# Nyström attention, ELU feed-forward and top-2 experts in one Trainium2 kernel: float32 transposes and landmark sums of batch 0 on TensorE, 32x32 Newton blocks, contiguous A parts, and a new order of all engines

## The chip, the cores and the metric

The kernel runs on one core of a Trainium2 chip. The metric is device time in microseconds (us), the median of several executions of the whole kernel; lower is better. The engines are named as the profile names them: PE is TensorE (PEld its weight loads), DVE VectorE, ACT ScalarE, POOL GpSimd, and SP the engine that issues the plain DMAs. Each engine works through its own instructions in order.

## What is computed

Three stages follow each other. Nyström attention has 4 batches, 8 heads, 576 tokens of 64 numbers and 32 landmarks, each of which is the mean of 18 successive tokens. Its output is a matrix x of 2304 tokens by 512, which goes through a feed-forward layer with ELU, and then through a router that sends each token to two of eight experts.

```python
q_lm = q.reshape(B, H, 32, 18, 64).mean(axis=3)          # same for k
A, Bm, C = sm(q, k_lm), sm(q_lm, k_lm), sm(q_lm, k)      # row softmaxes of scaled products
Z = Bm.T / (norm1(Bm) * norminf(Bm) + 1e-6)
for _ in range(6):
    Z = 2 * Z - Z @ Bm @ Z
x = A @ Z @ C @ v
h = x @ w_in                                             # 512 -> 2048
y = where(h > 0, h, exp(min(h, 0)) - 1) @ w_out          # 2048 -> 512
out = sum over the 2 best experts of weight * relu(y @ w1[e]) @ w2[e]
```

## The kernel before

**Number formats.** Most products run in float16 with every operand split into a high part and a remainder ("hi" and "lo"), three matmuls per product (hi hi, hi lo, lo hi). The splits are made by ACT (hi) and by DVE or POOL (lo). The weights w_in and w_out arrive as raw 32-bit words that four steps per tile turn into floats: `I.j.part` and `Wa.kk.part`, where part 0 runs on ACT, part 1 (line 256) and part 2 (line 257) on DVE, and part 3 on POOL (line 258). `Wb` then splits w_out into two float16 halves (line 289 on DVE).

**Attention.** Each of the 4 batches is worked on in two groups g of 4 heads. `lmsum` sums 18 tokens per landmark from the float32 q or k, on DVE (one reduction, line 318) or POOL (six additions). `xhi` (ACT) and `xlo` (DVE, line 364) split q and k. For batch 0, PE transposes the halves (`xtp`, line 370, 6 float16 blocks per call, 12 calls) and ACT or DVE copies them out of PSUM (`xte`, line 378); for batches 1 to 3 a DMA transposes them (`xtr`). The landmark sums are split (`lhi`, `llo`), transposed on PE (`ltr`) and copied out (`lcp`). Then come the three score products: `asmm` for A, `csmm` for C, `bmm` for B. A's softmax is a chain of steps between DVE, POOL and ACT (`astr`, `asmax`, `assub`, `asexp`, `assum`, `asmul`, `asback`), and its result is written as hi by ACT (`ashi`) and lo by DVE or POOL (`aslo`, line 591) into the tile AT, with a token order that strides through it.

**Newton.** The 32x32 matrices of the 8 heads are handled as block-diagonal 128x128 matrices of 4 heads. `btd` spreads the transpose of B into such blocks; `sqmm` squares one (line 452: two float32 matmuls of 128x128x128), `sqout` copies it to R, `umm` multiplies it into Y (line 524: two float32 matmuls with 32 columns), `uout` adds. Six rounds of each follow per batch. With `zcv` and `gmm`, Z, C v and w_in are folded into one matrix G per batch, whose halves are written by `ghi` (ACT) and `glo` (DVE, line 609).

**Feed-forward.** The 2304 tokens go in 6 chunks (512, 256, then four of 384), each with 16 blocks f of 128 hidden units. `L1.c.f` (line 634) forms h from AT and G, `X` takes exp on ACT, `T` the clipped part on ACT or DVE (line 656), `S` combines on DVE (line 660), `H` writes the float16 hi on ACT, `O` the lo on POOL (line 665), and `L2.c.f.t` (line 672) accumulates the outputs of 128 tokens each. The routing, the split of the expert weights and expert 0 come after; the remaining seven experts run in a loop of their own. `F.n` issues n idle matmuls of 128x128 on PE (line 646), which feed nothing.

**What sets the order.** One long string, ORDER, lists every step up to expert 0, as `batch:step.arguments` or `step.arguments`. The steps are issued in that order, and the scheduler is told to leave it alone on PE, DVE, ACT, POOL and SP, so the string fixes the row in each queue.

```python
with tc.manual_schedule(engines={ET.PE, ET.DVE, ET.Activation, ET.Pool, ET.SP}):
    do(ORDER)
```

Of the kernel before, what the change touches and what calls it, by code (L numbers as in the profile page):

```python
# [56 lines left out]
0:xtp.1.1.1 0:xte.1.1.1.A 0:nmm 0:btd.V I.7.2 0:nval Wl.7 Wa.0.0 0:sqmm.0 0:xtp.0.1.0 0:asmax.0 F.9 0:y0 I.1.1
0:xte.1.0.0.A 0:xtp.1.0.2 0:xtp.1.0.1 0:sqout.0 0:xte.1.1.2.V 0:sqmm.1 Wl.2 0:umm.0 0:xte.1.0.2.A I.3.1 wi.10
0:sqout.1 Wa.7.0 Wa.0.1 0:xtp.0.1.2 0:assub.0.G 0:xte.1.0.1.V I.7.0 I.4.1 0:sqmm.2 wi.9 0:asexp.0 I.0.3 0:csmm.1
0:sqout.2 Wa.0.2 Wl.3 I.1.2 wi.11 0:uout.0 0:csmm.0 Wa.4.3 Wa.0.3 I.3.0 Wb.0.0.V Wb.4.0.V 0:assum.0 0:xte.0.1.0.V  # L60
I.1.3 wi.12 Wa.7.1 0:xte.0.1.2.V 0:sqmm.3 0:sqout.3 0:umm.1 0:xtp.0.1.1 0:uout.1 wi.5 F.11 Wa.2.0 0:xte.0.1.1.A
0:umm.2 Wa.7.2 Wa.2.1 0:sqmm.4 F.9 0:csmax.0 0:csmax.1 Wa.1.1 Wa.2.2 Wa.1.2 Wa.7.3 0:asmul.0.G 0:csexp.0 I.11.0 I.12.0
F.10 I.2.2 0:csexp.1 Wa.3.0 I.8.1 I.11.1 0:asmm.1 I.9.0 0:uout.2 0:etrans.1 0:astr.1 0:etout.1 I.12.1 I.4.2 Wa.1.3
wi.13 Wl.5 I.4.0 0:umm.3 I.5.1 Wb.0.1.V 0:v 0:sqout.4 0:etrans.2 Wb.4.1.V 0:etrans.0 Wa.5.0 cl I.2.3 0:asmax.1 I.8.2
1:k.0 0:sqmm.5 0:sqout.5 0:uout.3 0:assub.1.G F.14 Wl.6 0:etout.2 0:asback.0 0:asexp.1 0:etout.0 Wa.2.3 Wb.1.0.V
Wb.2.0.V 0:ashi.0 0:umm.4 Wa.3.1 0:cssum I.3.2 Wb.7.0.V F.8 I.7.3 0:cv 0:uout.4 0:assum.1 0:cvout 0:umm.5 0:uout.5
I.3.3 I.4.3 I.5.0 1:q.0 0:asmul.1.V 0:ybd.V 0:aslo.0.G Wa.5.1 0:asback.1 0:zcv Wb.2.1.V 0:zout 0:ashi.1 1:lmsum.0.0.V
0:gmm.0 I.8.0 Wb.7.1.V 0:ghi.0.0 1:xhi.0.0 0:ghi.0.1 0:glo.0.1 F.36 0:aslo.1.G 0:glo.0.0 1:xlo.0.0 L1.0.0 I.10.0 X.0.0
I.5.2 T.0.0.V 1:xhi.1.0 S.0.0 L1.0.1 Wa.5.2 I.5.3 X.0.1 L1.0.2 wi.14 I.10.1 0:gmm.1 H.0.0 T.0.1.A Wa.3.2 Wb.1.1.V
O.0.0 S.0.1 1:xlo.1.0 I.13.0 L2.0.0.2 0:ghi.1.0 L2.0.0.3 X.0.2 Wa.3.3 H.0.1 0:ghi.1.1 1:q.1 1:lmsum.0.1.V L1.0.3  # L70
Wa.5.3 Wa.6.0 T.0.2.A L2.0.0.1 I.14.1 Wb.3.0.G O.0.1 S.0.2 1:lmsum.1.0.V 1:v 1:lhi.0 Wb.5.0.V X.0.3 0:glo.1.0 L2.0.0.0
L2.0.1.1 I.8.3 H.0.2 Wb.3.1.G T.0.3.A L2.0.1.0 1:xtr.0.0 0:glo.1.1 S.0.3 I.10.2 O.0.2 L2.0.1.3 1:xhi.0.1 Wb.5.1.V
1:llo.0 L1.0.5 L1.0.4 wi.15 I.9.1 consts 1:ltr.0 L2.0.2.3 I.9.2 H.0.3 1:k.1 X.0.5 O.0.3 1:lcp.0.A X.0.4 1:xlo.0.1
I.11.2 T.0.5.A I.11.3 L2.0.1.2 L2.0.2.0 T.0.4.V Wa.6.1 L2.0.3.3 S.0.4 I.9.3 L2.0.2.2 H.0.4 L2.0.3.2 I.10.3 S.0.5
L2.0.2.1 1:xtr.1.0 1:xtr.0.1 L2.0.3.1 L1.0.6 L1.0.7 O.0.4 I.14.2 I.14.0 H.0.5 1:lmsum.1.1.V 0:gmm.2 Wa.6.2 L2.0.4.3
I.15.0 1:xhi.1.1 X.0.6 0:ghi.2.1 O.0.5 0:ghi.2.0 Wa.6.3 L2.0.3.0 1:xlo.1.1 Wl.9 T.0.6.A L2.0.4.0 1:lhi.1 X.0.7
0:glo.2.0 L2.0.4.2 L2.0.5.2 S.0.6 Wb.6.0.V H.0.6 0:glo.2.1 Wl.8 Wa.9.0 O.0.6 Wa.9.1 1:llo.1 1:csmm.0 1:xtr.1.1 Wa.9.2
I.14.3 1:csmax.0 I.12.2 I.13.1 L2.0.4.1 L1.0.8 T.0.7.A Wb.6.1.V L2.0.5.3 X.0.8 Wl.12 Wa.8.1 I.15.1 1:csexp.0 L2.0.5.0
S.0.7 L2.0.5.1 L2.0.6.0 H.0.7 1:ltr.1 L2.0.6.3 T.0.8.A 1:lcp.1.V I.13.2 O.0.7 1:bmm Wa.8.2 L1.0.9 I.12.3 1:bmax Wa.8.0
X.0.9 1:csmm.1 L2.0.6.1 Wa.9.3 1:csmax.1 L2.0.6.2 L2.0.7.2 Wl.13 L2.0.7.1 1:bex T.0.9.A I.15.2 S.0.9 Wa.8.3 1:csexp.1  # L80
L2.0.7.0 I.15.3 1:asmm.0 Wa.12.0 1:bnorm 1:astr.0 L1.0.10 1:etrans.0 1:nmm I.13.3 Wl.11 Wb.8.0.V Wb.8.1.V 1:btd.A
# [95 lines left out]
EV.4.1 EA.0.1 EV.0.1 E1.2.1 EV.1.1 E1.6.1 E1.3.1 LW.0.1 EA.2.1 EA.6.1 EV.2.1 EV.6.1 LX.1.0 EA.3.1 ES.1 EA.7.1 ES.2
EV.3.1 EV.7.1 E2.3 E2.4 EO.4 PD.2.3 EO.3 LW.1.0 ES.3 ES.4
"""


# [953 lines left out]
```

## Time and profile before

| | us |
| --- | --- |
| median of 3 runs | 844.60 |
| lowest and highest of them | 843.96 and 846.16 |
| the profiled execution, its own time | 843.73 |
| its span | 842.1 |

The span is what the profile shows from the first to the last instruction, 1.6 us less than the time of that same execution. The start of the span, up to 64.4 us, is the attention of batch 0 and the first weight conversions. From 64.4 to about 150 us chunk 0 of the feed-forward runs beside the attention of batch 1; to about 450 us the other chunks run beside batches 2 and 3; and then come the experts. In the views a busy time is what an engine's instructions covered, "x" is their count, and PEclk is the granted TensorE clock as a share of full speed.

### The profile page before, as it was taken

The numbers are of one execution on the slowest core, as the hardware profiler recorded it, in microseconds if no ns is written. First come the engines' busy times: TensorE is split into PE (matmuls) and PEld (weight loads), VectorE is DVE, ScalarE is ACT, GpSimd is POOL, SyncE is SP. The second block draws the span as 40 slices with busy tenths as digits, with TensorE's granted clock in tenths as the row PEclk, the third lists the DMA queues.
The fourth block names the chain that finished last, engine by engine and source line by source line (L and its number), as shares of the span: only waits on it lengthen the run. The fifth ranks groups of instructions, "written<-read, shape, count | busy, mean of one in ns | idle before, by whom it ended". The sixth has DMA issues, their size and how long they took to land. (4 is left out here: it accounts for less than half of the span.)

```text
span 842.1 us, 15270 instructions
## 1 busy us (share of the span) xinstructions
...
## 2 busy tenths in 40 slices
...
GB/s 334 305 168 192 184 299 343 154 214 219 111 218 98 181 81 127 76 110 55 190 101 201 144 182 122 144 161 91 183 81 160 139 110 189 49 11 39 223 107 36
DMA packets 136971, 129.11 MB, mean 153 GB/s; under 512 B 100581, under 2 KB 103653, under 8 KB 136800
## 3 DMA queue, kind: packets, MB, share of 16 engines
...
HBM read 70.64 MB, written 39.90 MB: 131 GB/s over the span
## 5 line engine op out<-in xcount | busy, mean ns | idle before, releaser
L931 PE MATMUL ey<-w,eh 128*128 128x512 f16 (+1 forms) x960 | 208.8, 379 | 0.0
L672 PE MATMUL y<-wout,g 128*128 128x512 f16 x864 | 207.1, 379 | 1.6 <-DVE wout L289 0.9
L901 PE MATMUL eh<-xT,w 128*128 128x304 f16 (+2 forms) x1536 | 200.4, 293 | 0.0
L911 DVE SCALAR_TENSOR_TENSOR eh<-eh,eh 128x304 f16<-128x304 f32 (+2 forms) x128 | 59.8, 471 | 228.0 <-ACT eh L217 228.0
L901 PEld LDWEIGHTS <-w 128*128 128x128 f16 x1536 | 149.9, 98 | 49.6
L931 PEld LDWEIGHTS <-eh 128*128 128x128 f16 (+1 forms) x960 | 98.7, 103 | 106.9
L939 POOL DMA_INDIRECT acc<-eo,tk x35 | 55.9, 1597 | 280.2 <-ACT eo L217 144.1
L665 POOL TENSOR_TENSOR g<-e,g 128x384 f16<-128x384 f32 (+2 forms) x96 | 100.4, 1049 | 129.8 <-ACT g L217 113.8
L672 PEld LDWEIGHTS <-g 128*128 128x128 f16 x864 | 81.3, 99 | 94.6 <-issue 9.3
L634 PE MATMUL h<-AT,G 128*128 128x192 f16 (+3 forms) x768 | 110.2, 289 | 7.9 <-DVE e L660 5.0
L217 ACT ACTIVATE eh<-eh 128x304 f16<-128x304 f32 (+2 forms) x128 | 53.8, 424 | 118.0 <-PE eh L901 111.3
L634 PEld LDWEIGHTS <-G 128*128 128x128 f16 x768 | 64.2, 99 | 49.4 <-issue 11.2
L868 DVE SCALAR_TENSOR_TENSOR w<-ew,w 128x1024 f16<-128x1024 f32 x64 | 78.2, 1223 | 22.8 <-ACT w L217 22.8
L217 ACT ACTIVATE eo<-ey,ws 128x512 f32<-128x512 f32 (+1 forms) x35 | 23.8, 687 | 135.1 <-PE ey L931 135.1
L660 DVE SCALAR_TENSOR_TENSOR e<-e,h 128x384 f32<-128x384 f32 (+2 forms) x96 | 52.6, 550 | 33.8 <-ACT e L217 26.0
L217 ACT ACTIVATE e<-h 128x384 f32<-128x384 f32 (+2 forms) x96 | 47.4, 495 | 47.3 <-PE h L634 22.0
L217 ACT ACTIVATE w<-ew 128x1024 f16<-128x1024 f32 x64 | 66.9, 1047 | 0.0
L217 ACT ACTIVATE g<-e 128x384 f16<-128x384 f32 (+2 forms) x96 | 49.8, 520 | 31.7 <-DVE e L660 18.6
L840 POOL DMA_INDIRECT xs<-rows,pos x36 | 36.5, 1014 | 31.4 <-DVE count L832 20.5
L217 ACT ACTIVATE e<-e 128x384 f32<-128x384 f32 (+2 forms) x57 | 30.0, 526 | 0.9
L656 DVE TENSOR_SCALAR e<-e 128x384 f32<-128x384 f32 (+2 forms) x39 | 19.2, 493 | 17.0 <-ACT e L217 16.9
L609 DVE SCALAR_TENSOR_TENSOR G<-pg,G 128x512 f16<-128x512 f32 x32 | 21.6, 689 | 7.7 <-ACT G L217 7.7
...
## 6 DMA issues: line engine op xcount, KB each, us to landing
...
v<-in_v_dram SPq DMA_DIRECT2D x4, 1152.0 KB, 11.0
...
```

The costliest lines, as they stand in the source:

```text
L217: return A.activation(o, i, f, **kw)
L609: V.scalar_tensor_tensor(gt[:, g, 1, fs], X["pg"][g], S_G, gt[:, g, 0, fs], op0=ALU.mult, op1=ALU.subtract)
L634: T.matmul(p[:, c0:c0 + n], GT[b, f // 8][:, g, x, fs], AT[b][:, g, y, o:o + n], start=(i == 0), stop=(i == 5))
L660: V.scalar_tensor_tensor(x[1], x[1], x[2], x[0], op0=ALU.mult, op1=ALU.max)
L665: G.tensor_tensor(out=HT[c, f][:, 1], in0=x[1], in1=HT[c, f][:, 0], op=ALU.subtract)
L672: T.matmul(YP[c, t], h[:, x, 128 * t:128 * t + 128], WOUT[f][:, y], start=(f == 0 and i == 0), stop=(f == 15 and i == 2))
L840: n = nc.gpsimd.indirect_dma_start(out=xs[:, :], out_offset=bass.IndirectOffsetOnAxis(ap=R["pos"][:, i // 2, i % 2:i % 2 + 1], axis=0), in ...
L868: V.scalar_tensor_tensor(dst[1][:, ks, :], t, scale, dst[0][:, ks, :], op0=ALU.mult, op1=ALU.subtract)
L901: T.matmul(p, W1T[e][x][:, d, 128 * f:128 * f + 128], XT[e][y][:, d, s0:s0 + n], start=(i == 0 and d == 0), stop=(i == 2 and d == 3))
L911: V.scalar_tensor_tensor(h[:, 1, s0:s0 + n], EP[e, f, s0], 0.0, h[:, 0, s0:s0 + n], op0=ALU.max, op1=ALU.subtract)
L931: T.matmul(p, EH[e, f][:, x, 128 * j:128 * j + live(j)], W2T[e][y][:, f, :], start=(f == 0 and i == 0), stop=(f == 7 and i == 2))
L939: nc.gpsimd.indirect_dma_start(out=acc[:, :], out_offset=bass.IndirectOffsetOnAxis(ap=TK[e][:live(j), j:j + 1], axis=0), in_=EO[e, j], in_ ...
```

## The change

1. **Batch 0's inputs.** The float32 q and k are transposed directly on PE: `xtp` now makes 3 float32 blocks per call (12 calls). The split follows behind the transposition, out of PSUM: `xth` writes hi on ACT, `xtl` lo on DVE. The landmark sums of batch 0 are formed on PE too: `lmmm` adds pairs of tokens with 9 float32 matmuls against the identity, 4 calls, and `lmadd` (DVE) adds what is left. `xhi`, `xlo`, `xte` and `lmsum` are no longer used for batch 0.
2. **Newton.** `btd` is gone. `sqmm` and `umm` issue 8 matmuls of 32x32x32, one for each head, and R shrinks to 32 columns per group.
3. **A's parts** are written contiguously, so that a batch's tokens come in another order. The noise of the router is therefore loaded by 16 DMAs (`nz.b.j`) in place of one, and the token numbers take six more small DVE operations in `consts`.
4. **The remainder O** of ELU may run on DVE. Of chunk 0's 16 it does so for 11; over all chunks DVE has 54 of 96. T of chunk 0 runs on ACT throughout (before, 10 on ACT and 6 on DVE). `aslo` of batch 1 moves from DVE to POOL, and other steps of A's softmax are dealt out anew between DVE and POOL.
5. **The overflow branch**, which runs only when an expert gets more than 608 tokens, uses plain loads and a selecting matmul instead of indirect DMAs. It isn't executed on these inputs.
6. **ORDER** is written anew throughout. The first loads are weights, then k and q in turn.

```diff
-F.127 0:q.0 0:xhi.0.0 0:k.0 0:xtp.0.0.0 0:k.1 0:xhi.1.1 0:q.1 Wl.4 0:xlo.0.0 0:lmsum.0.0.G 0:lmsum.1.0.V 0:xte.0.0.0.A
...
+F.127 wi.2 wi.0 0:k.0 wi.6 0:q.0 0:xtp.0.0.0 I.0.0 0:xtp.1.0.0 I.6.0 I.0.1 0:xth.0.0.0 0:lmmm.0.0 0:q.1 I.6.1 I.6.2
...
+    ident32 = cst.tile([128, M], F32, name="ident32")
+    V.tensor_reduce(out=ident32, in_=ident.rearrange("p (h m) -> p m h", h=4), axis=AX.X, op=ALU.add)
...
+        def lmmm(s_, g):
+            x = (QS, KS)[s_][b, g]
+            p = X["ls", s_, g] = small("", None, 256 * s_ + 128 * g, 128)
+            for r in range(SEG // 2):
+                T.matmul(p, ident, x[:, 2 * D * r:2 * D * r + 2 * D], start=(r == 0), stop=(r == SEG // 2 - 1))
+        def lmadd(s_):
...
+            p = small("", None, 256 * s_, 256).rearrange("p (g u d) -> p g d u", g=2, u=2)
+            V.tensor_reduce(out=X["lmr"][:, s_], in_=p, axis=AX.X, op=ALU.add)
...
-            p = X["xp", n, g, j] = s1(f"xp{b}{n}{g}{j}", ("a", "y")[n], F16)
-            for c in range(6):
-                T.transpose(p[:, 128 * c:128 * c + 128],
-                            X["x", n, g].rearrange("p x n -> p (x n)")[:, 128 * (6 * j + c):128 * (6 * j + c + 1)], ident16)
-        def xte(n, g, j, e):
+            p = X["xp", n, g, j] = s1(f"xp{b}{n}{g}{j}", ("a", "y")[n])
+            for c in range(3):
+                T.transpose(p[:, 128 * c:128 * c + 128], (QS, KS)[n][b, g][:, 128 * (3 * j + c):128 * (3 * j + c + 1)], ident)
+        def xth(n, g, j):
...
+            act(xT[n, g][:, 3 * j:3 * j + 3].rearrange("p c n -> p (c n)"), X["xp", n, g, j][:, :384], scale=S_QK)
+        def xtl(n, g, j):
+            hi, lo = (xT[n, g][:, o + 3 * j:o + 3 * j + 3].rearrange("p c n -> p (c n)") for o in (0, 9))
+            V.scalar_tensor_tensor(lo, X["xp", n, g, j][:, :384], S_QK, hi, op0=ALU.mult, op1=ALU.subtract)
...
-        def btd(e):
-            X["BTd"] = tile_a([128, 2, 4, M], "k1")
-            spread(X["BTd"], X["BB"][:, 1], 2, e)
...
+        def blocks(p, x, y):
+            for g in range(2):
+                for h in range(4):
+                    sl = slice(32 * h, 32 * h + 32)
+                    T.matmul(p[sl, g], x[sl, g], y[sl, g], start=True, stop=True)
         def sqmm(i):
-            p = X["pq", i] = small(f"pq{b}{i}", n_tag, 0, 256).rearrange("p (g m) -> p g m", g=2)
-            for g in range(2):
-                x = X["BTd"][:, g].rearrange("p h m -> p (h m)") if i == 0 else R[i - 1][:, g]
-                T.matmul(p[:, g], x, x, start=True, stop=True)
+            p = X["pq", i] = small(f"pq{b}{i}", n_tag, 0, 64).rearrange("p (g m) -> p g m", g=2)
+            x = X["BB"][:, 1] if i == 0 else R[i - 1]
+            blocks(p, x, x)
         def sqout(i):
             p = X["pq", i]
-            r = R[i] = sa.tile([128, 2, 128], F32, tag="R", bufs=NR, name=f"R{b}{i}")
+            r = R[i] = sa.tile([128, 2, M], F32, tag="R", bufs=NR, name=f"R{b}{i}")
...
         def umm(i):
...
-            for g in range(2):
-                T.matmul(p[:, g], R[i][:, g], Y[:, g], start=True, stop=True)
+            blocks(p, R[i], X["Y"])
...
         def ashi(g):
...
-            act(AT[b][:, g, 0, :].rearrange("p (m c u) -> p u c m", u=2, c=9), X["ay", g])
+            act(AT[b][:, g, 0, :].rearrange("p (c u m) -> p u c m", u=2, c=9), X["ay", g])
         def aslo(g, e=V):
-            hi, lo = (AT[b][:, g, i, :].rearrange("p (m c u) -> p u c m", u=2, c=9) for i in range(2))
+            hi, lo = (AT[b][:, g, i, :].rearrange("p (c u m) -> p u c m", u=2, c=9) for i in range(2))
...
         if part == "O":
-            G.tensor_tensor(out=HT[c, f][:, 1], in0=x[1], in1=HT[c, f][:, 0], op=ALU.subtract)
+            e.tensor_tensor(out=HT[c, f][:, 1], in0=x[1], in1=HT[c, f][:, 0], op=ALU.subtract)
...
-        nc.sync.dma_start(noise_t, noise.rearrange("(t p) e -> p t e", p=128))
+    def noise_load(b, j):
+        r0 = (j - SEG * b) % 4
+        n, t0 = len(range(r0, SEG, 4)), (SEG * b + r0) // 4
+        nc.sync.dma_start(noise_t[32 * j:32 * j + 32, t0:t0 + n],
+                          noise.rearrange("(b m r) e -> b m r e", b=B, r=SEG)[b, :, r0::4])
```

Three places of the new order follow. In a row, a name is that of a tile, the digits behind its underscore count tiles, and the sizes are those of the output.

**The start, on DVE.** Before, rows 8 to 16 of DVE's queue; `x` holds the two float16 halves, `k10` the landmark sums, `T` the transposed halves, `lm` the split sums:

```order
L364 SCALAR_TENSOR_TENSOR x000_236<-q00_234,x000_236 128x1152
L318 TENSOR_REDUCE k10_256<-k00_238 128x64
L318 TENSOR_REDUCE k10_256<-q01_251 128x64
L378 COPY T000_266<-xp0001_268 128x768
L256 TENSOR_SCALAR woc4_277<-wo4_253 128x512
L332 SCALAR_TENSOR_TENSOR lm0_257<-k10_256,lm0_257 128x2x64 x2
L364 SCALAR_TENSOR_TENSOR x101_249<-k01_247,x101_249 128x1152
L364 SCALAR_TENSOR_TENSOR x100_290<-k00_238,x100_290 128x1152
L332 SCALAR_TENSOR_TENSOR lm0_257<-k10_256,lm0_257 128x2x64 x2
```

After, rows 11 to 21:

```order
L262 SCALAR_TENSOR_TENSOR wi12_242<-wi12_242,win1_256 128x512
L262 SCALAR_TENSOR_TENSOR wi00_238<-wi00_238,win0_250 128x512
L400 SCALAR_TENSOR_TENSOR T000_259<-xp0000_246,T000_259 128x384
L400 SCALAR_TENSOR_TENSOR T100_279<-xp0100_252,T100_279 128x384
L261 TENSOR_SCALAR win0_250<-wi02_236 128x512
L261 TENSOR_SCALAR woc4_294<-wo4_276 128x512
L262 SCALAR_TENSOR_TENSOR wi02_236<-wi02_236,win0_250 128x512
L261 TENSOR_SCALAR woc0_311<-wo0_282 128x512
L400 SCALAR_TENSOR_TENSOR T000_259<-xp0001_297,T000_259 128x384
L261 TENSOR_SCALAR win1_256<-wi10_285 128x512
L344 TENSOR_REDUCE k10_362<-nb0_261 128x128
```

The landmark sums moved from rows 9 and 10 to row 21 (one small reduction out of the PSUM tile `nb0`), behind weight conversions and the first remainders of the transposed blocks.

**The start, on PE.** After, the rows behind the first 127 idle matmuls, where before six float16 transposes of `x000` stood:

```order
L390 MATMUL xp0000_246<-ident_69,q00_244 128x128 x3
L390 MATMUL xp0100_252<-ident_69,k00_240 128x128 x3
L336 MATMUL nb0_261<-q00_244,ident_69 128x128 x9
L390 MATMUL xp0101_289<-ident_69,k00_240 128x128 x3
L390 MATMUL xp0001_297<-ident_69,q00_244 128x128 x3
L336 MATMUL nb0_261<-q01_271,ident_69 128x128 x9
L390 MATMUL xp0002_316<-ident_69,q00_244 128x128 x3
L336 MATMUL nb0_261<-k00_240,ident_69 128x128 x9
L336 MATMUL nb0_261<-k01_287,ident_69 128x128 x9
L390 MATMUL xp0110_340<-ident_69,k01_287 128x128 x3
```

All four landmark sums now stand in PE's row between the transposes, ahead of the scores.

**Chunk 0, on DVE.** Before, rows 108 to 114 (rows 104 and 105 are the two of `G` that release the first `L1`); `e` is the ELU tile, `h` the product in PSUM, `wo` and `win` weight words:

```order
L656 TENSOR_SCALAR e_0_1005<-e_0_1005 128x512
L660 SCALAR_TENSOR_TENSOR e_0_1005<-e_0_1005,h_0_997 128x512
L257 SCALAR_TENSOR_TENSOR wo_772<-wo_772,woc_794 128x512
L256 TENSOR_SCALAR win_706<-wi_543 128x512
L257 SCALAR_TENSOR_TENSOR wo_595<-wo_595,woc_724 128x512
L289 SCALAR_TENSOR_TENSOR wout_630<-wo_403,wout_630 128x512
L660 SCALAR_TENSOR_TENSOR e_1_1021<-e_1_1021,h_1_1012 128x512
```

After, rows 113 to 120 (the same two of `G` are rows 108 and 109); `g` is the float16 output of ELU:

```order
L680 SCALAR_TENSOR_TENSOR e_1_1088<-e_1_1088,h_1_1069 128x512
L384 SCALAR_TENSOR_TENSOR x_1084<-q_974,x_1084 128x1152
L680 SCALAR_TENSOR_TENSOR e_0_1096<-e_0_1096,h_0_1076 128x512
L262 SCALAR_TENSOR_TENSOR wi_396<-wi_396,win_550 128x512
L685 TENSOR_TENSOR g_0_1118<-e_0_1096,g_0_1118 128x512
L629 SCALAR_TENSOR_TENSOR G_1000<-pg_1109,G_1000 128x512
L629 SCALAR_TENSOR_TENSOR G_1000<-pg_1108,G_1000 128x512
L685 TENSOR_TENSOR g_1_1100<-e_1_1088,g_1_1100 128x512
```

T (line 656) left DVE's row, O (line 685) joined it, and fewer conversions stand between the ELU steps.

## Rows read from the trace of the kernel before

**Rows 1.** The head of the profile's page.

```profile
span 842.1 us, 15270 instructions
```

**Rows 2.** Windows by stage: start:end, length, busy us per engine (xinstructions), PEclk, DMA, GB/s.

```profile
0.00:64.40 64.40, 45.30 (x642) 38.69 (x643) 54.46 (x114) 40.86 (x66) 32.54 (x34) 0.81 0.81 264
64.40:150.00 85.60, 76.35 (x614) 35.74 (x615) 82.79 (x132) 61.65 (x112) 52.71 (x46) 0.98 0.88 262
150.00:450.00 300.00, 293.84 (x2504) 164.01 (x2503) 191.79 (x534) 186.30 (x368) 144.01 (x184) 1.00 0.52 139
450.00:780.00 330.00, 330.00 (x2047) 204.19 (x2046) 106.55 (x184) 111.35 (x186) 54.47 (x34) 1.00 0.60 123
780.00:842.10 62.10, 50.64 (x312) 30.82 (x310) 11.35 (x21) 7.47 (x17) 11.54 (x16) 0.93 0.38 122
```

**Rows 3.** DVE by line and shape, 0 to 64.4 us: xcount | busy, mean ns | idle.

```profile
L318 DVE TENSOR_REDUCE k<-q 128x64 f32<-128x1152 f32 x2 | 4.4, 2184 | 0.0
L364 DVE SCALAR_TENSOR_TENSOR x<-q,x 128x1152 f16<-128x1152 f32 x3 | 4.2, 1390 | 3.7 <-ACT x L217 3.7
L257 DVE SCALAR_TENSOR_TENSOR wo<-wo,woc 128x512 int32<-128x512 int32 x5 | 3.3, 681 | 0.0
L378 DVE COPY T<-xp 128x768 f16<-128x768 f16 x6 | 3.2, 539 | 1.0 <-PE xp L370 1.0
L576 DVE TENSOR_TENSOR ax<-ax,amx 128x576 f32<-128x576 f32 x1 | 2.6, 2630 | 0.0
```

**Rows 4.** The start: a window, and PE's timeline (start, us, what [idle before <-releaser]).

```profile
0.00:12.00 12.00, 10.03 (x131) 10.04 (x133) 6.60 (x15) 3.63 (x4) 7.43 (x15) 1.00 0.85 324
...
20.31 0.92 PE L400 MATMUL pa<-T,lT 64*32 64x288 f16 x24
```

**Rows 5.** PE's timeline, 43 to 45 us: float32 transposes and float32 matmuls.

```profile
43.56 1.05 PE L489 MATMUL pe<-ident,E 128*96 128x128 f32 x8
44.46 0.61 PE L452 MATMUL nb<-R 128*128 128x128 f32 x4
44.90 0.28 PE L646 MATMUL warm<-ident 128*128 128x128 f16 x2
```

**Rows 6.** Timeline at the end of batch 0's attention.

```profile
57.76 2.73 ACT L217 ACTIVATE AT<-ay 128x576 f16<-128x576 f32 x1
...
60.57 3.04 POOL L591 TENSOR_TENSOR AT<-ay,AT 128x576 f16<-128x576 f32 x1 [4.33 <-ACT AT L217]
...
64.40 0.82 PE L634 MATMUL h<-AT,G 128*128 128x512 f16 x3 [0.79 <-DVE G L609]
```

**Rows 7.** DVE by line and shape, 64.4 to 150 us.

```profile
L257 DVE SCALAR_TENSOR_TENSOR wo<-wo,woc 128x512 int32<-128x512 int32 x10 | 10.2, 1032 | 0.0
...
L591 DVE TENSOR_TENSOR AT<-ay,AT 128x576 f16<-128x576 f32 x2 | 5.4, 2696 | 0.0
...
L656 DVE TENSOR_SCALAR e<-e 128x512 f32<-128x512 f32 x6 | 3.6, 593 | 0.0
...
L576 DVE TENSOR_TENSOR ax<-ax,amx 128x576 f32<-128x576 f32 x1 | 0.7, 717 | 0.0
```

**Rows 8.** POOL by line and shape, 64.4 to 150 us.

```profile
L665 POOL TENSOR_TENSOR g<-e,g 128x512 f16<-128x512 f32 x15 | 20.7, 1383 | 17.5 <-issue 9.2 <-ACT g L217 8.3
```

**Rows 9.** PE by line and shape, 210 to 450 us.

```profile
L524 PE MATMUL pu<-Y,R 128*128 128x32 f32 x48 | 6.5, 259 | 2.1 <-ACT R L217 2.1
...
L502 PE MATMUL pcv<-v,ET 96*32 96x64 f32 x192 | 3.1, 220 | 0.0
```

**Rows 10.** Weight loads of PE, from the page's costliest groups.

```profile
L634 PEld LDWEIGHTS <-G 128*128 128x128 f16 x768 | 64.2, 99 | 49.4 <-issue 11.2
```

**Rows 11.** Windows of 2 us in the start, for the granted clock.

```profile
18.00:20.00 2.00, 0.72 (x29) 0.69 (x30) 2.00 (x4) 1.70 (x4) 0.73 (x1) 0.50 1.02 385
...
42.00:44.00 2.00, 1.04 (x9) 0.91 (x9) 2.00 (x5) 2.00 (x5) 0.63 (x1) 1.00 1.10 248
```

More of the change, by code (lines that the diff above doesn't have):

```diff
@@ L57 @@
[L57 to L81, printed above, removed]
@@ L177 @@
[L177 to L178 removed]
+F.127 wi.2 wi.0 0:k.0 wi.6 0:q.0 0:xtp.0.0.0 I.0.0 0:xtp.1.0.0 I.6.0 I.0.1 0:xth.0.0.0 0:lmmm.0.0 0:q.1 I.6.1 I.6.2
+I.0.2 Wl.4 0:xtl.0.0.0 0:xth.1.0.0 0:xtl.1.0.0 Wl.0 I.2.1 wi.4 0:k.1 0:xtp.1.0.1 I.2.0 Wa.4.1 0:xth.1.0.1 0:xtp.0.0.1
+0:lmmm.0.1 I.2.2 Wa.0.0 0:xth.0.0.1 I.0.3 wi.3 0:xtp.0.0.2 0:lmmm.1.0 0:lmmm.1.1 Wa.0.1 0:xtl.0.0.1 0:xtp.1.1.0 I.4.1
```

276 lines of the change are left out of this document (157 added, 119 removed).

## The prediction

> **What bounds the kernel now.** I read the windows by stage first, and in each the gap between its length and the busy time of PE and of the next busiest engine. From 450 to 780 us PE has no gap at all, and from 150 to 450 us only 6.2 us of 300, so there a change counts only if it takes work off PE [rows 2]. From 64.4 to 150 us PE is busy 76.35 of 85.6 us and DVE 82.79: DVE sets the pace, and 9.25 us of PE can be won at most. Up to 64.4 us DVE works 54.46 us and idles 9.94, while much of PE's busy time is idle matmuls, which produce nothing. The end of that stage is the first L1 whose operands DVE wrote last: PE waited 0.79 us for DVE's G there [rows 6]. The tail from 780 us issues the same work in both kernels and I leave it. So the change has three places to act: DVE's load up to 64.4, DVE's load in chunk 0, and PE's matmuls in batches 2 and 3.
>
> **The start.** DVE loses four xlo (4 x 1.39 = 5.6), two landmark reductions (4.4), six xte copies (3.2) and one asmul that took 2.6 [rows 3]: 15.8 us. It gains twelve xtl of 384 columns. The trace has no such operation reading float32 from PSUM; by columns from xlo it would take 0.46, and a remainder of 512 columns took 0.68 [rows 3]. I take 0.57 and get 6.8, ends 5.5 and 8.2. Two lmadd reduce 256 numbers per partition where lmsum reduced 1152: by columns 0.49 each, 1.0. The new order puts three more conversions of 0.68 ahead of G, 2.0. The small rest (btd and one w_out split away, an identity and a copy more) is set to nothing. The sum is 15.8 - 9.8 = 6.0 us less on DVE, 48.5 us busy, and 58.4 us with the same 9.94 us idle.
>
> Against it, the landmark sums come later. The first 127 idle matmuls fill PE to 12.0 as before (131 matmuls, 10.03 us, 0.077 each) [rows 4]. Behind them stand, up to the first score product of A, seven xtp, four lmmm and 15 idle matmuls. Eight float32 transposes took 0.90 from their start to the next matmul, 0.11 each, and two float32 matmuls of 128 columns 0.44, 0.22 each [rows 5]. That gives 7 x 3 x 0.11 + 4 x 9 x 0.22 + 15 x 0.077 = 2.3 + 7.9 + 1.2 = 11.4, and the scores at 23.4 where they were at 20.31 [rows 4]: 3.1 later. The data are just in time. The ten loads up to k.1 are six of 512 KB and four of 576 KB, 5.5 MB, or 17.0 us at the 324 GB/s of the first window [rows 4], and PE wants k.1 at 12 + 7.7 = 19.7. DVE has conversions to fill the 3.1 us, but its row is fixed and I charge them in full, with 0.9 for the last chain, where the waits follow each other closely. The first L1 then starts at 58.4 + 3.1 + 0.9 = 62.4: **gain 2.0**, ends -0.5 (the upper xtl price, and one more wait of a microsecond) and 6.0 (nothing charged). What hides A's parts there: the strided writes took 2.73 on ACT and 3.04 on POOL, and POOL ended 0.8 us before L1 [rows 6]. Contiguous ones are late next if they are no cheaper; by O's contiguous 1.38 for 512 columns on POOL [rows 8], 1.56 for 576, they leave room.
>
> **Chunk 0.** DVE gains eleven O. A subtraction of two float32 operands took 0.717 for 576 columns there [rows 7], so 0.64 for 512: 7.0 us. It gains six small operations for the token numbers, 1.0 (ends 0 and 4.3, at 0.717 each), and two w_out splits, 1.4. It loses two strided A remainders (5.4), six T (3.6) [rows 7] and about two weight conversions (1.9). Together -1.5. The wo conversions took 1.032 here against 0.681 in the start [rows 3, 7]: 10 x 0.35 = 3.5 us that look like the price of POOL at work beside them. POOL loses 11 x 1.383 = 15.2 and gains two A remainders, 3.1: 12.1 of its 52.7 us, 23% [rows 2, 8], so I take 0.8 of the 3.5. **Gain 2.3**, ends -2 and 9.25, all of PE's idle time. T moves to ACT, which is busy 61.65 of 85.6; six T more, less four or so of A's work, fit.
>
> **Newton.** In batches 2 and 3 PE sets the end, so 12 calls each of sqmm and umm count there. sqmm takes 0.44 to the next start, 0.17 less than its own 0.61 since ends overlap [rows 5]. umm is 6.5 / 12 = 0.54 [rows 9], and 0.37 less the same overlap. Blocks of 32 rows and columns don't stand in the trace. The nearest are the small float32 matmuls of C v: two records per matmul, 192 in 3.1 us, 16.1 ns each [rows 9]. Eight matmuls are 16 records, 0.26. Saved: 12 x (0.18 + 0.11) = 3.5, ends 9.7 (both calls vanish) and a loss, below. **Gain 3.5.** Latency matters in batches 0 and 1, where DVE has other work beside them: nothing.
>
> The sixteen noise loads are 15 more DMAs in SP's queue, behind which later weight loads wait; no stage waits for DMA longer than for its engines, so nothing, and a part of the fourth rival if not.
>
> Sum: 2.0 + 2.3 + 3.5 = 7.8. From the profiled execution's 843.73 (its span is 842.1 [rows 1]) that is 835.9; the median of the runs is 0.87 above that execution, so **836.8**, the likeliest's own range 831 to 842.
>
> **The rivals.**
> *PE closes up in chunk 0.* O on DVE ends the trip to POOL, whose O waited 8.3 us for its input, and only PE's own work is left. Start 4, chunk 7, Newton 3.5: 14.5, so 830. For it: both engines' busy times are near the length, and less work on DVE frees both. Against: DVE loses only 1.5 there.
> *O on DVE runs into POOL.* One subtraction on DVE, beside one on POOL, took 2.63 in the start and 0.717 in chunk 0 [rows 3, 7]. At 1.0 for each of the eleven, 4 us are lost: 841. At 2.34 for each it would be 18.7, which is what the far end looks like. Against: five O are left on POOL of chunk 0, so fewer collide.
> [...]
> *New waits between 150 and 450 us.* The order of every engine is new, and PE's 6.2 idle us there are few. If they become 13, as in a stretch half as well packed, 7 us go: 844, no change. For it: DVE's O and 16 more DMAs stand in the way of steps that PE needs. Against: DVE is busy 191.79 of 300 there [rows 2].
> [...]
> [...]
> *The blocks don't overlap, slower.* If each of the eight waits for its weight load of 99 ns [rows 10], a call takes 0.79 in place of 0.41: 24 x 0.38 = 9.1 lost, not 3.5 won, so 843.7 - 4.3 + 9.1 + 0.9 = 849. It decides from 0.7 per call. Against: C v's small matmuls have their own loads and still take 16.1 ns.
>
> **How the numbers follow.** Forecast 0.44; PE closes up 0.13; O into POOL 0.15; new waits 0.13; half clock 0.09; no overlap 0.06. The first three are faster by over 0.3% (2.5 us, about what a measurement of this kernel can tell from no change): 0.72. The fourth is within it, 0.13. The last two are slower, 0.15. The predicted time is the likeliest's, 836.8. The range goes from 827, the lower end of the second case, to 847, which leaves out most of the two slower ones and little else.
>
> **What would show it.** The first L1 at 62.4 (start), scores at 23.4, xtl near 0.57 each. In chunk 0, O on DVE at 0.64, wo conversions below 1.032, and PE's idle time near 7 us. sqmm and umm calls of about 0.25 us. PE idle near 6 us from the end of chunk 0 to the experts. I would be wrong if the first L1 came after 65, if O cost over 1 us, or if PE had gaps in batches 2 and 3 that it has not now.

## The result and the profile after

The changed kernel takes 830.6 us (828.38 to 831.71, 4 runs) against 844.42 for the kernel before: a ratio of 0.9829, 95% interval 0.9809 to 0.9849. A second series of the same kernel gave 829.39 (828.31 to 830.21, 5 runs), ratio 0.9821 (0.9807 to 0.9834). The forecast was 836.8, with a range of 827 to 847: the direction and the range held, but where 13.8 us were gained the terms of my sum made 7.8.

The windows of the changed kernel, cut at three events (first L1 with its operands complete, last L2 of chunk 0, last L2 of chunk 5); columns as in [rows 2]:

```profile
0.00:62.37 62.37, 48.13 (x822) 41.03 (x824) 45.03 (x118) 34.08 (x70) 21.73 (x26) 0.89 0.87 286
62.37:151.08 88.71, 83.87 (x868) 37.60 (x868) 79.93 (x150) 66.97 (x132) 51.12 (x50) 1.00 0.83 242
151.08:412.64 261.56, 256.38 (x2504) 136.68 (x2503) 178.35 (x503) 159.27 (x333) 84.86 (x119) 0.99 0.57 147
```

The last two stages of the kernel before, cut at the same events. [Rows 2] and the prediction end them at 150 and 450 us, but by these events chunk 0 ends at 160.65 and the first expert matmul starts at 422.96:

```profile
64.40:160.65 96.25, 87.00 (x711) 40.83 (x712) 89.92 (x143) 70.21 (x129) 60.60 (x54) 0.98 0.82 247
160.65:422.74 262.09, 256.78 (x2227) 144.11 (x2226) 169.56 (x463) 168.19 (x336) 129.09 (x164) 1.00 0.52 139
```

The lengths tell where the time went: the start gained 2.0 us, chunk 0 7.5, and the 260 us of chunks 1 to 5 only 0.5. The experts are the same to 0.03 us, from their first matmul to their last. The rest, 1.9 us, lies behind the last matmul, where I had seen nothing. Together that is 12.0 us before rounding, the difference of the two spans; the profiled execution of the changed kernel is the longest of its four, so the medians are 13.8 apart. In chunk 0 DVE's busy time fell by 10 us, to 79.93, though the change put eleven O on it, about as much work as it took off it (T, A's parts); PE's idle time fell from 9.25 to 4.84.

The waits of PE in chunk 0, before and after (PE line <- what it waited for: us, times, longest), show one place where this counts:

```profile
PE h L634 <- DVE G L609: 2.9, 2, 2.1
```

```profile
PE h L654 <- DVE G L629: 0.2, 1, 0.2
```

In the kernel before, PE ran at half clock right behind the longer of those two waits, from 79.4 to 82.8 us (granted clock 0.50), busy all the time; the changed kernel's PE has no half-clock stretch in chunk 0 (granted 1.00 against 0.98). At half the pace those 3.4 us do 1.7 us of work, so about 1.7 of the 7.5 go with that stretch, by estimate.

In DVE's rows of that window the operations that the change left alone got shorter. Before and after, each from its own window of chunk 0 (line and shape, xcount | busy, mean ns):

```profile
L257 DVE SCALAR_TENSOR_TENSOR wo<-wo,woc 128x512 int32<-128x512 int32 x11 | 10.9, 1000 | 0.0
...
L256 DVE TENSOR_SCALAR woc<-wo 128x512 int32<-128x512 int32 x9 | 7.4, 827 | 0.0
L257 DVE SCALAR_TENSOR_TENSOR wi<-wi,win 128x512 int32<-128x512 int32 x8 | 6.9, 858 | 0.0
```

```profile
L685 DVE TENSOR_TENSOR g<-e,g 128x512 f16<-128x512 f32 x11 | 8.8, 803 | 1.5 <-ACT g L220 1.4
...
L262 DVE SCALAR_TENSOR_TENSOR wo<-wo,woc 128x512 int32<-128x512 int32 x9 | 7.2, 797 | 0.0
...
L262 DVE SCALAR_TENSOR_TENSOR wi<-wi,win 128x512 int32<-128x512 int32 x7 | 4.7, 684 | 0.0
...
L261 DVE TENSOR_SCALAR woc<-wo 128x512 int32<-128x512 int32 x9 | 3.7, 420 | 0.0
```

Why they are shorter is seen in single rows. The timeline of the changed kernel at 65 us, DVE and POOL:

```profile
65.57 1.04 POOL L263 TENSOR_TENSOR win<-wi 128x512 int32<-128x512 int32 x1
65.59 1.56 DVE L294 SCALAR_TENSOR_TENSOR wout<-wo,wout 128x512 f16<-128x512 f32 x1
66.57 1.49 POOL L263 TENSOR_TENSOR wo<-wo 128x512 int32<-128x512 int32 x1
...
67.08 0.67 DVE L680 SCALAR_TENSOR_TENSOR e<-e,h 128x512 f32<-128x512 f32 x1
67.68 1.59 DVE L384 SCALAR_TENSOR_TENSOR x<-q,x 128x1152 f16<-128x1152 f32 x1
```

The first DVE row starts 0.02 us behind a POOL operation and takes 1.56 instead of 0.68: POOL's remaining 1.02 and then 0.54 of its own. The last one starts 0.38 us ahead of the end of a POOL operation and takes 1.59 instead of 1.35. The one between, whose second operand h lies in PSUM, runs beside POOL at its full pace. One row shows the other way too: the POOL operation at 66.57, which started while the first DVE row was still at work, took 1.49 where the shortest of its kind takes 1.03. So the two DVE rows that start while POOL works are longer by 0.88 and 0.24 us, where POOL's operations had 1.02 and 0.38 left.

Which kind that is, all rows up to the experts tell, in both traces. Of the conversions, copies and two-operand steps whose operands all lie in SBUF, 75 start at least 0.3 us before the end of a POOL operation (indirect DMAs and memsets left out), and 70 of them are held, longer by at least half of what that operation had left; 68 of the 70 are longer by all of it but 0.10 to 0.15 us. One SBUF operand was enough here: all 11 weight conversions of lines 256 and 261 among them are held. Of 158 operations that read PSUM, none is; and of 63 reductions, transposes, reciprocals and searches, which read SBUF as well, none either.

I call what an operation takes above the fast tenth of its line and shape in both traces its excess, where that is more than 0.1 us (A's parts, whose layout changed, are left out). The excess of DVE's operations in chunk 0 was 17.2 us before and is 7.0 now; in the start 7.0 and 1.9; in chunks 1 to 5 12.3 and 5.6. In the start and in chunk 0 all of it, in both kernels, is in operations that started beside one of POOL's.

### The profile page after: what moved, and what is told of

Its sections match the earlier page's. It is cut to its first block, busy times and chain, and to the rows that moved or that the text cites. A ratio compares the mean times of both kernels' runs of the same rounds, so it can differ in the third digit from the quotient of the medians.

```text
span 830.0 us, 16481 instructions
## 1 busy us (share of the span) xinstructions
PE 795.4 (96%) x6725; PEld 465.2 (56%) x6726; DVE 434.2 (52%) x1033; ACT 387.1 (47%) x749; POOL 228.5 (28%) x255
## 4 chain that ended last, share of the span: by engine, by line
PE 81%; DVE 9%; ACT 3%; DMA 2%; issue 2%; POOL 1%; SPq 0%; POOLq 0%; DVEq 0%; ACTq 0%
PE ey L963 25%; PE eh L933 23%; PE y L692 18%; PE h L654 8%; PE pg L621 1%; DMA q<-in_q_dram 1%; PE nb L336 1%; ACT L220 1%; DVE e L680 1%; ACT e L220 1%; DVE k L323 1%; DMA wo<-in_moe_w_out_dram 1%; POOL xs L872 1%; PE pe L511 1%; DVE g L685 1%
## 5 line engine op out<-in xcount | busy, mean ns | idle before, releaser
L692 PEld LDWEIGHTS <-g 128*128 128x128 f16 x864 | 80.3, 98 | 91.5 <-issue 10.2
L900 DVE SCALAR_TENSOR_TENSOR w<-ew,w 128x1024 f16<-128x1024 f32 x64 | 78.0, 1223 | 25.3 <-ACT w L220 22.6
L685 POOL TENSOR_TENSOR g<-e,g 128x384 f16<-128x384 f32 (+2 forms) x42 | 41.6, 991 | 140.8 <-ACT g L220 139.0
L685 DVE TENSOR_TENSOR g<-e,g 128x384 f16<-128x384 f32 (+2 forms) x54 | 31.5, 588 | 12.2 <-ACT g L220 11.9
L220 ACT ACTIVATE e<-e 128x384 f32<-128x384 f32 (+2 forms) x62 | 32.5, 531 | 0.9
L263 POOL TENSOR_TENSOR win<-wi 128x512 int32<-128x512 int32 x16 | 18.8, 1184 | 33.7 <-DVE wi L262 29.3
## 6 DMA issues: line engine op xcount, KB each, us to landing
wi<-in_moe_w_in_dram SPq DMA_DIRECT2D x16, 512.0 KB, 10.2
```

The lines of the kernel that those rows point to most:

```text
L220: return A.activation(o, i, f, **kw)
L263: lambda: G.tensor_tensor(out=hi if dst is None else dst, in0=hi, in1=lo, op=ALU.add)), hi.bitcast(F32)
L685: e.tensor_tensor(out=HT[c, f][:, 1], in0=x[1], in1=HT[c, f][:, 0], op=ALU.subtract)
L692: T.matmul(YP[c, t], h[:, x, 128 * t:128 * t + 128], WOUT[f][:, y], start=(f == 0 and i == 0), stop=(f == 15 and i == 2))
L900: V.scalar_tensor_tensor(dst[1][:, ks, :], t, scale, dst[0][:, ks, :], op0=ALU.mult, op1=ALU.subtract)
```

## The experiments

All stages are read off each run's trace at the same events. "Start" is the start of the first L1 record, "chunk 0" that of its last L2, "experts" that of the first expert matmul. Some traces have two to four records of L1 and then a wait for the rest of its operands; with these complete, L1 starts at 64.40 before, at 62.37, 62.17 and 62.87 in the changed kernel (its two series, and the one with the old branch, which differs only in that branch), at 69.06 with the float16 split, 68.66 with strided parts and 61.43 in the last row.

| kernel | start | chunk 0 | experts | span | median of its runs |
| --- | --- | --- | --- | --- | --- |
| before | 63.02 | 160.65 | 422.96 | 842.1 | 844.4 |
| changed, first series | 61.63 | 151.08 | 412.85 | 830.0 | 830.6 |
| changed, second series | 61.40 | 149.58 | 410.00 | 827.2 | 829.4 |
| changed, old overflow branch | 62.87 | 149.76 | 409.51 | 828.6 | 830.3 |
| changed, wide Newton products | 64.14 | 153.14 | 413.47 | 830.7 | 832.2 |
| changed, O on POOL | 61.22 | 151.16 | 418.64 | 836.3 | 839.9 |
| changed, more POOL work | 63.27 | 157.36 | 418.34 | 835.5 | 837.3 |
| changed, landmark sums on DVE | 65.51 | 152.95 | 412.59 | 829.8 | 830.8 |
| changed, float16 split first | 68.34 | 155.77 | 415.73 | 832.9 | 835.7 |
| changed, strided A parts | 64.99 | 159.35 | 427.38 | 844.6 | 847.5 |
| before, new overflow branch | 62.71 | 160.68 | 422.98 | 840.2 | 841.9 |
| before, Newton blocks | 63.35 | 157.84 | 420.76 | 839.9 | 841.9 |
| before, O of chunk 0 on DVE | 62.97 | 166.13 | 430.81 | 849.9 | 851.5 |
| before, four parts without the order | 60.64 | 163.17 | 432.65 | 849.9 | 849.5 |

### The end: the overflow branch

```diff
 before:  -  nc.gpsimd.indirect_dma_start(out=base, out_offset=None, in_=out[:, :], in_offset=ix, ...)
          +  nc.sync.dma_start(base, out[128 * t:128 * t + 128])   # and the rest of the new branch
 changed: the same, backwards
```

> The kernel before with the new overflow branch alone. Theory (the branch costs its end 1.9 us): 842.5, with nothing changed up to the last matmul. Rival: 844.4.

> The changed kernel with the old overflow branch (indirect DMAs on GpSimd), which isn't executed on these inputs. Theory (the end pays for a branch that isn't run: in the trace of before GpSimd waits on one more semaphore and runs a 1.8 us INC_SWDGE_SEM before its last DRAIN, which the changed kernel has not): the stretch behind the last matmul is 1.9 us longer, 832.5. Rival (the tail only varies from run to run): 830.6.

The kernel before with the new branch took 841.89 us, a ratio of 0.9972 (0.9960 to 0.9984), about 2 us. Up to the last expert matmul the two traces differ by 0.03 us. The last row of POOL's timeline and the head of the page, of the kernel before (its span is 842.1) and of that variant:

```profile
831.71 0.93 POOL L953 DMA_INDIRECT out_dram<-eo,tk  x1 [4.13 <-DVE eo L951]
```

```profile
span 840.2 us, 15268 instructions
...
831.73 0.93 POOL L953 DMA_INDIRECT out_dram<-eo,tk  x1 [4.13 <-DVE eo L951]
```

From the start of that last scatter to the end of the span it is 10.3 us with the old branch and 8.5 with the new one. In the instructions behind it, POOL has one of 1.81 us (INC_SWDGE_SEM) with the old branch, ahead of a drain of 6.7 us, and none with the new. The changed kernel with the old branch shows the same 10.3 (scatter at 818.24, span 828.6), and the changed kernel 8.5 (821.58, 830.0). So the old branch, which is never entered and holds indirect DMAs of POOL, costs 1.9 us at the end in both kernels. In the runs of the changed kernel this can't be told apart: 830.26 with the old branch, 830.6 and 829.39 without, since its middle varies by as much.

### Newton: blocks of 32

```diff
 before:  -  T.matmul(p[:, g], x, x, start=True, stop=True)              # two of 128x128x128
          +  T.matmul(p[sl, g], x[sl, g], y[sl, g], start=True, stop=True)   # eight of 32x32x32, no btd
 changed: the same, backwards, with btd behind nmm
```

> The kernel before with the 32x32 Newton blocks alone (no btd). Theory 1 (as predicted: PE sets the end in batches 2 and 3, and DVE in chunk 0): 4.0 less between the end of chunk 0 and the experts, nothing in chunk 0: 840.4. Theory 2 (the Newton time counts in chunk 0 too, 3.4 there): 837. Rival (PE waits elsewhere for as much): 844.4.

> The changed kernel with the Newton products of before (two matmuls of 128x128, spread by btd), all else as in the changed one. Theory 1 (PE is nearly full from the first L1 on, so all of the 7.4 us that the trace shows count): 838. Theory 2 (only batches 2 and 3 count): 834.6. Rival (waits take it up either way): 831.

The blocks alone brought the kernel before to 841.88, ratio 0.9974 (0.9964 to 0.9984), 2.1 us. The wide products took the changed kernel to 832.21, 0.9849 (0.9830 to 0.9867), 1.6 and 2.8 us more than its two series, though the interval still overlaps theirs. In the kernel before, the size is half of what I expected, and the place is the opposite: by the table the gain is 2.8 us at the end of chunk 0 and none in chunks 1 to 5. In the changed kernel the first L1 comes 1.3 to 2.7 later with the wide products than in the three traces without them. There the Newton chain of batch 0 is what the rest waits for: its last step on DVE ends at 52.83 with them, and at 51.13 to 51.44 without.

Chunks 1 to 5 show why PE won so little. PE's timeline of the kernel before (start, us), a squaring between two groups of L2 matmuls and transposes:

```profile
212.15 0.81 PE L672 MATMUL y<-wout,g 128*128 128x512 f16 x3
212.79 0.61 PE L452 MATMUL pq<-k 128*128 128x128 f32 x4
213.24 1.04 PE L489 MATMUL pe<-ident,E 128*96 128x128 f32 x8
```

The same with blocks:

```profile
209.33 0.81 PE L677 MATMUL y<-wout,g 128*128 128x512 f16 x3
210.07 0.33 PE L454 MATMUL pq<-BB 32*32 32x32 f32 x16
210.33 1.08 PE L496 MATMUL pe<-ident,E 128*96 128x128 f32 x8
...
216.50 0.33 PE L454 MATMUL pu<-Y,R 32*32 32x32 f32 x16 [2.02 <-ACT R L217]
216.76 2.62 PE L677 MATMUL y<-wout,g 128*128 128x512 f16 x6
```

The blocks themselves take 0.26 (210.07 to 210.33), as I had worked out from C v; the wide product takes 0.45 (212.79 to 213.24). But three L2 matmuls take 0.64 up to a wide product and 0.74 up to the blocks: 0.09 us pass before a block product starts behind a large matmul, nearly the same in each call that follows one without a wait. So most squarings save 0.09 and not 0.18, most umm 0.01 and not 0.11, and the 24 calls, added up row by row, 1.9 us and not 3.5. Two things took those. One more wait of 0.6 us arose (for DVE's Y). And from 216.9 to 220.3, right behind a wait of 2.0 us for ACT's R, PE ran at half clock: six L2 matmuls took 2.55 us instead of 1.28. The window:

```profile
216.90:220.30 3.40, 3.40 (x24) 1.17 (x23) 2.34 (x14) 3.40 (x3) 0.64 (x3) 0.50 0.02 5
```

The first series of the changed kernel has one such stretch too, from 197.3 to 200.7 (granted clock 0.50), behind a wait of 2.1 us, and its second series none (1.00 there), though it waits 2.4 us at the same place. With that stretch go 1.4 of the 2.85 us by which these two profiles differ. Nor does the kernel before slow down behind the same wait for R, which is 2.1 us there:

```profile
219.53 0.63 PE L524 MATMUL pu<-Y,R 128*128 128x32 f32 x4 [2.10 <-ACT R L217]
```

So such a wait can be followed by half clock, and what decides it these runs don't show.

### O on DVE

```diff
 changed: -  e.tensor_tensor(out=HT[c, f][:, 1], ...)      # 54 of 96 on V
          +  G.tensor_tensor(out=HT[c, f][:, 1], ...)
 before:  -  O.0.0   +  O.0.0.V                            # 11 of chunk 0's 16
```

> The changed kernel with all 96 remainders O on POOL as before, the order otherwise the same. Theory 1 (O on DVE pays because POOL's long operations block DVE's operations with two SBUF operands: DVE's excess over the shortest of each shape, 7 us in chunk 0 of the changed kernel and 17 before, goes back up to 12 or more, and L2 waits for POOL): chunk 0 is 3 to 6 longer, 835. Theory 2 (DVE is the bound by its own busy time, which falls by 7.5 in chunk 0): 829 or less.

> The kernel before with 11 of chunk 0's O on DVE (those of the changed kernel), nothing else. Theory 1 (locks: the 7.0 us on DVE are paid back by fewer collisions with POOL): DVE's excess in chunk 0 falls from 17 to about 10, the time stays at 842 to 845. Theory 2 (as predicted, a plain sum on the engine that sets the pace): 7 more, 851.

Both results are far from small, and neither is what I expected of chunk 0. With all O on POOL the changed kernel takes 839.94 (0.9947, 0.9932 to 0.9962), 9.3 and 10.5 us more than its two series, but chunk 0 is as long as ever. DVE lost 7.5 us of work there and its excess rose from 7.0 to 10.9. The loss is in chunk 1 (4.6 against the first series) and at the end of chunk 5 (4.3), where POOL's row also holds the routing. In chunk 1 it is a wait of 2.7 us for `spacer` and a half-clock stretch behind it (186.1 to 189.5, about 1.7 by estimate: six L1 matmuls take 2.13 us in it and 1.14 after it). The waits of PE, chunks 0 to 5 (PE line <- what it waited for: us, times, longest):

```profile
PE h L650 <- DVE e L676: 3.8, 5, 1.2
PE y L688 <- POOL spacer L867: 3.7, 2, 2.7
PE y L688 <- POOL g L681: 1.6, 2, 1.1
```

`spacer` is a step behind each scatter of the routing; an O that stands behind it in POOL's row comes late for L2 (the 1.6 us for g).

In the kernel before, eleven O on DVE cost 7.5 us (851.49, ratio 1.0077, 1.0061 to 1.0094), 5.5 of them in chunk 0. DVE's excess stayed at 17.0, so the theory of locks, by which fewer collisions with POOL pay for the eleven, fell here, and the plain sum on the engine that sets the pace, 7 foreseen, held but for 1.5 us. About as much as it missed came in chunk 2, with a half-clock stretch (226.8 to 230.2) that the kernel before doesn't have there (granted 1.00; the mean over the run is 0.977 here and 0.979 before); that the total is 7.5 is in part this accident.

### Does POOL's work alone slow DVE?

```diff
+    def pz():
+        G.tensor_tensor(out=PZ[0], in0=i, in1=i, op=ALU.add)   # 128x256, i is ident, repeated
 ORDER: "pz pz" behind each O.0.f
```

> The changed kernel with 32 more POOL operations in chunk 0 (two of 128x256 behind each O, some 0.7 us each, of SBUF operands; nobody reads what they write). POOL is busy 50 of 89 us there. Theory 1 (a POOL operation blocks the DVE operations that start beside it): DVE's excess in chunk 0 rises from 7 to 12 or more, and chunk 0 is 4 to 6 longer, 835 to 837. Theory 2 (POOL has room and only its own row counts): 830.6, at most 1 more.

It took 837.30 (0.9917, 0.9901 to 0.9934), 7 us more, as the first theory says: 4.6 in chunk 0, and 1.6 in the start, ahead of any added operation; there the changed kernel's own three traces lie 1.5 apart. POOL's work was 25.3 us more (the first row below); DVE's own operations were the same, and their excess rose from 7.0 to 14.9. The groups of this run, to be held against those of the changed kernel above (wo 797, wi 684):

```profile
L691 POOL TENSOR_TENSOR pz<-ident 128x256 f16<-128x256 f32 x32 | 25.3, 791 | 1.4
```

```profile
L262 DVE SCALAR_TENSOR_TENSOR wo<-wo,woc 128x512 int32<-128x512 int32 x9 | 8.8, 976 | 0.0
...
L262 DVE SCALAR_TENSOR_TENSOR wi<-wi,win 128x512 int32<-128x512 int32 x7 | 5.9, 857 | 0.0
```

POOL's own row cost one wait of PE (1.2 us, for A's lo part). Not all of the 8 us of excess came through, since DVE has some room in the changed kernel (79.93 of 88.71 us).

### The start

```diff
 landmark sums on DVE:     lmmm: pass
                        -  V.tensor_reduce(out=X["lmr"][:, s_], in_=p, ...)
                        +  for g in range(2): lmsum(s_, g, V)
 float16 split first:      xtp: xhi and xlo ahead of a tile's first transpose, 6 float16 blocks
                           xth, xtl: a copy out of PSUM, half of them on ACT, half on DVE
```

> The changed kernel with batch 0's landmark sums on DVE (four reductions over 18 tokens, where the changed one has two short ones) and without the 36 float32 matmuls that made them. Theory 1 (DVE's busy time sets the first L1): DVE works 7.9 us more before it, the first L1 is 5 to 8 later, 835 to 838. Theory 2 (the landmarks' latency over PE set it: DVE idled 3.0 us for them, and the scores came at 28.0 where I forecast 23.4): part is given back, L1 at most 3 later, 832.

> The changed kernel with batch 0's q and k split into float16 halves before the transposes, as before (72 float16 transposes, copies half on ACT and half on DVE), the order otherwise kept, the split put ahead of the first transpose of each. DVE works 2.2 us more in the start by the rows (5.6 + 3.2 - 6.6), ACT 2.3. Theory 1 (busy time): first L1 2 to 3 later, 832.5. Theory 2 (latency: the scores now wait for split, transpose and copy in a row): 5 or more later, 836. Rival (the new order alone made the start shorter): 830.

With the sums on DVE the first L1 came 4 us later than in the two series, but 1.5 were given back by chunk 2 against the second, and the runs show no difference (830.82; 0.9831, 0.9807 to 0.9855, against 0.9829 and 0.9821). The order has room for most of DVE's 7.9 us: at the experts that trace is 2.6 us behind the second series and 0.3 ahead of the first, so this part of the change is not told apart from nothing. The split ahead of the transposes costs more: 835.70 (0.9893, 0.9871 to 0.9914), the first L1 6.9 later than in the second series. DVE's busy time up to there grew by 3.9 us (48.92 against 45.03), and it waited for ACT's halves:

```profile
L384 DVE SCALAR_TENSOR_TENSOR x<-q,x 128x1152 f16<-128x1152 f32 x3 | 4.1, 1357 | 11.1 <-ACT x L220 11.1
```

So the delay is latency ahead of the first scores (32.6 here, 28.0 in the changed kernel) as much as work.

### Contiguous A parts, and the parts without the order

```diff
 changed: -  AT[b][:, g, 0, :].rearrange("p (c u m) -> p u c m", ...)    # ashi, aslo the same
          +  AT[b][:, g, 0, :].rearrange("p (m c u) -> p u c m", ...)
          -  noise_load in 16 pieces, tokid by six operations   +  one DMA, one iota
 before:  the parts Newton, A, O on DVE and overflow branch, in the order of before
```

> The changed kernel with A's parts written with strides and the tokens in their own order, so with one noise DMA and without the six small DVE operations; aslo stays where the changed kernel has it. A write takes 2.7 on ACT for 0.7 and 3.0 on POOL for 1.4. Theory 1 (a longer POOL operation blocks DVE, and the last A part ends late for the first L1): start 1 to 3 later, chunk 0 another 2: 834. Theory 2 (ACT and POOL have room): 830.

> The kernel before, in its own order, with the parts of the change that need no new order: Newton blocks, contiguous A parts, O on DVE for the same 54 blocks, new overflow branch. Theory 1 (the order is most of the gain: O on DVE in rows not arranged for it cost 7.9 in chunk 0 alone): 845 to 850. Theory 2 (the parts are the gain): 836 or less.

Strided A parts in the new order are the most expensive thing I undid: 847.51, slower than the kernel before (1.0031, 1.0020 to 1.0042), 17 us above the changed kernel, though neither ACT nor POOL is busy all the time (72.5 and 55.0 of 93.7 us in chunk 0). Timeline at the first L1 of that run, and PE's longest waits from 60 to 200 us:

```profile
63.08 2.72 ACT L220 ACTIVATE AT<-ay 128x576 f16<-128x576 f32 x1
...
65.88 2.72 POOL L611 TENSOR_TENSOR AT<-ay,AT 128x576 f16<-128x576 f32 x1 [3.50 <-ACT AT L220]
...
68.66 1.89 PE L654 MATMUL h<-AT,G 128*128 128x512 f16 x8 [2.43 <-POOL AT L611]
```

```profile
PE h L654 <- POOL AT L611: 6.3, 3, 2.5
PE pg L621 <- ACT Z L220: 2.8, 1, 2.8
```

In the changed kernel the two writes take 0.69 and 1.40 us and PE never waits for them. Here the hi part (2.72) and then the lo part (2.72) follow each other ahead of L1, in the start and again as batch 1 begins, at the end of chunk 0. Against the second series the loss is 3.6 us by the first L1 record, 6.2 more up to the end of chunk 0 (2.4 of them the wait at 68.66) and 7.6 in chunks 2 and 3. In these two PE doesn't wait for A's parts but for DVE (G 2.6, the ELU steps 2.8), whose excess in chunks 1 to 5 is 10.6 instead of 5.6; that the longer POOL writes cause it is likely and not shown by itself. Half-clock stretches from 146.1 to 152.9 and 320.2 to 323.6, which the changed kernel doesn't have there (granted 1.00 in both; its chunk 0 has 1.00 and this run's 0.96), make some 4 of the 17, by estimate: PE was busy 7.7 us in them, at half the pace.

The four parts together in the order of before cost 5.0 us (849.53; 1.0048, 1.0031 to 1.0065). They shorten the start by 2.4 us, then lose 4.9 in chunk 0, where DVE with eleven O in its row is busy 93.00 of 101.8 us and its excess is 16.6, and 7.2 in chunks 1 and 2. Half-clock stretches (97.3 to 100.7, 128.0 to 134.8 and 227.0 to 230.4, where the kernel before has one of 3.4 us; granted 0.95 in chunk 0 against 0.98) make up to 5 us of these losses, by estimate. Not in this run are batch 0's transposes and sums, T on ACT and A's steps dealt out anew. So these four parts alone don't bring the gain of 13.8: it takes the rows laid out for them, with T and A's steps moved; and in that order two of the parts can't be missed. The new order with the old parts was not run.

## Why the prediction was right and where it wasn't

**The start**: 2.0 foreseen, 2.0 measured (first L1 at 62.37 against 62.4), but by two errors that cancel, which is luck. The scores came at 28.0 and not at 23.4: PE's row was done with the sums at 21.4, but the second reduction of the sums stood in DVE's row behind conversions and began at 25.12, and PE waited for what follows it. PE's timeline:

```profile
22.40 0.50 PE L390 MATMUL xp<-ident,k 128*128 128x128 f32 x3
26.04 0.23 PE L360 MATMUL nb<-ident,lm 128*128 128x128 f16 x1 [3.14 <-DVE T L400]
26.57 0.91 PE L360 MATMUL nb<-ident,lm 128*128 128x128 f16 x7 [0.30 <-DVE lm L352]
28.00 0.92 PE L420 MATMUL pa<-T,lT 64*32 64x288 f16 x24 [0.52 <-DVE lT L364]
```

And DVE had 3.5 us less to do than my 48.5 (45.03): its excess fell by 5.1, of which I had counted only what stood in asmul's 2.6 us, some 1.9. The prices were good: xtl 0.548 (0.57), lmadd 0.42 (0.49), a call of xtp 0.33, a float32 matmul 0.11 for each of its two records.

**Chunk 0**: 2.3 foreseen, 7.5 measured. That DVE sets the pace there was right, and so was O's own price (most of the eleven took 0.68; I had 0.64, from a row that I read as a subtraction and that is asmul's multiplication). The step that failed is the collisions: I took 0.8 us of 3.5, in proportion to POOL's busy time. But the collisions did not fall in proportion to busy time: eleven O off POOL left the excess at 17.0 in the old order, and the four parts at 16.6. By the rows it is a matter of which starts beside which, and the new rows set that: there the excess is 7.0, 10.2 us less. Newton's blocks, to which I had given nothing there, brought 2.8 in the run of their own.

**Newton in batches 2 and 3**: 3.5 foreseen, 1.9 by PE's rows and none in the length of chunks 1 to 5 in the run of their own: the term was missized by the 0.09 us ahead of each block product, and a half-clock stretch and a wait took the remainder. The price of the blocks, 0.26, was right.

**The end**: nothing foreseen, 1.9 measured. I left the tail out because it issues the same work, and with it the branch that isn't entered.

So that the range held is in part luck as well: chunk 0 gave 5.2 us more than its term and the end 1.9, chunks 1 to 5 gave 3.0 less.

**The rivals.** The time is that of "PE closes up in chunk 0" (830), and chunk 0 has its 7 us, with PE's idle time down to 4.84, well past the 7 of the forecast; its other terms (4 in the start, 3.5 in Newton) are not there. New waits in chunks 1 to 5 did not come: PE idles 5.18 us there against 5.31. Half clock in the start, to which I gave 0.09, did not come behind the first idle matmuls: from 11.4 to 22.8 us, with seven groups of float32 transposes among the sums, the granted clock was 1.00, and it first fell behind the wait of 3.14 us, to 0.50 from 26.6 to 30.0:

```profile
11.40:22.80 11.40, 11.40 (x108) 11.14 (x108) 6.17 (x12) 3.91 (x9) 3.08 (x3) 1.00 1.03 411
```

No run shows that term: the 0.09 was my estimate, and this window, in which the transposes are mixed with matmuls, shows 1.00 in its place. The rows at 65 us show what a collision costs, 1.56 for 0.68, and no delay for the operation with one operand in PSUM (0.67). I had counted such collisions, from the 2.63 and 0.717 of [rows 3, 7], in the loss that O might bring, and with 0.8 us at most in the gain that a new order might.
